# Split weights stored in device memory and fetched again as parts, in a kernel of attention and two feed-forward layers

## The chip, the cores and the metric

One Trainium2 chip, one NeuronCore. The metric is the device time of one execution in microseconds (us): 1044.35 us for the kernel before, the median of three runs. Five engines take part. TensorE (PE, with its weight loads as PEld) multiplies into PSUM banks; VectorE (DVE) and ScalarE (ACT) read those banks; GpSimd (POOL) works on SBUF alone; SyncE (SP) issues nearly all DMAs, in the order in which they stand in its program. Every engine takes its own instructions in order, so one that waits holds up all that stand behind it.

## The reference, cut to what matters

```
scores = scale * q @ k.T + decay           # 4 batches, 8 heads, 576 rows, head size 64
attn   = softmax(causal(scores)); x = attn @ v        # 2304 tokens, 512 wide
xn     = x / sqrt(mean(x*x) + 1e-6) * rms_g
x      = (silu(xn @ w_gate) * (xn @ w_val)) @ w_out   # 512 -> 1536 -> 512
out    = silu(x @ w_in) @ w_out2                      # 512 -> 2048 -> 512
```

The inputs q, k, v, f and rms_g are float32. The five weight matrices come as float64, which no engine multiplies: the kernel turns each 64-bit word into a float32 by integer operations ("decoding").

## The kernel before, in words

Every product of the two layers is made to nearly float32 accuracy from two parts of each operand, a high part (h) and the rounding rest, the low part (l): three matmuls, h by h, l by h and h by l, add up in one PSUM bank (`terms`, line 720). In names of tiles the last letter tells the part (`b11h`, `t4l`), and weights are `wh`, `wl` (input side) and `woh`, `wol` (output side).

The program runs in five stages. Attention comes first. Then each of the two layers goes over the tokens in two phases, tokens 0 to 1279 and 1280 to 2303: stage 2 is the gated layer's first phase, stage 3 its second, stage 4 the second layer's first phase, stage 5 its second. In each stage the loop `for g in range(0, NF, G)` of `layer` takes two column blocks of 128 at a time; such a step is called a group here. The gated layer has six groups in a stage, each with two input weights (gate and val), and the second layer eight groups, each with one. Stage 2 multiplies plainly. Stages 3 to 5 take a 2 by 2 block scheme with seven products (`p1`, `p2`, `p6`, `p5`, `p7`, `p4`, `p3`), for which the weights' four blocks `a11, a12, a21, a22` and four sums of blocks (`s1` to `s4`) are wanted; the first half of the group uses the tiles with `a11, a12, s2, s1` (here the first part) and the second half those with `a21, a22, s3, s4` (the second part). In stage 3 a group's order on PE is: 12 matmuls of p1, 12 of output blocks, p2, output, p6, output, p5, output, p7, p4, p3. "Output blocks" are the multiplications by `woh` and `wol` of the group before, which are put off into the next group (`pending`).

In the products, ACT copies a bank three times while it goes on filling (line 732: `u1` after p1, `u2` after p6, `u3` after p7, and p4 can only go on after the copy of `u3`); DVE adds such copies to other banks (line 737); ACT applies silu (line 830); DVE or POOL multiplies gate by val (line 837); ACT and DVE split the result (lines 639, 640).

Weights come in through `weights`: the first time, a 512 KB DMA into a tile `st`, one ACT and four DVE operations (lines 143 to 147) and a store of the float32 block to a `kept` tensor in device memory; the second time, a DMA of the `kept` block. After that, every time, `unit_in` makes the four sums on POOL (line 162), the high parts on ACT (165) and the low parts on DVE or POOL (166); `unit_plain` (183, 184) and `unit_out` (193, 194) do the same without sums. So in stages 3 and 5, where weights come the second time, sums and splits are made anew. `unit_ahead` decodes blocks of `w_in` during stage 3: eight of its sixteen (`AHEAD_OF`).

Buffers that set the order: four tiles each of `wh` and `wl`, three each of `woh` and `wol`, three tiles `f` for weights in float32, nine tiles `c`. The order of each engine's instructions is set when the program is built, by a scheduler that works with its own estimates; waits on semaphores keep it right at run time.

## Time and profile before

| | us |
|---|---|
| median of three runs (lowest to highest) | 1044.35 (1044.26 to 1046.67) |
| the profiled execution, whole | 1049.42 |
| its span, first to last instruction | 1047.6 |
| PE busy in the span | 1027.0 (98%) |
| DVE, ACT, POOL busy | 762.8, 566.0, 408.7 |
| stages 1 to 5, by the profiled execution | 224.7, 239.1, 191.1, 211.4, 181.3 |
| DMA moved | 104.29 MB, mean 100 GB/s |

A busy PE is not yet a PE at its pace: matmuls overlap, and the profile models their ends. What PE loses is seen better where two starts stand farther apart than usual, and in the list of what ended its waits. In the notation, "PE t L720 <- ACT c L732: 3.0, 3, 1.5" says that matmuls of line 720 into a tile `t` waited for ACT's writing of `c` in line 732, 3.0 us in total, three times, 1.5 us at the longest. PEclk is the granted share of TensorE's full clock.

### The profile page before, as it was taken

Reading aid. Unit: us, or ns where it says so; the run is one execution under the profiler, and the core shown is the slowest. Engines: PE = TensorE matmul, PEld = TensorE weight load, DVE = VectorE, ACT = ScalarE, POOL = GpSimd, SP = SyncE. Lnnn points to the kernel's source line nnn. Section 1 sums busy time; section 2 is a strip of 40 time slices with the busy share of each in tenths; the row PEclk is TensorE's granted clock in tenths of the full one; section 3 lists DMA queues with packets and bytes.
Section 4 is the critical chain, followed back from the end, with each engine's and each line's share of the span. In section 5 each row is a group of like instructions: output and inputs, shape, how many; then the busy total and the mean of one; then the engine's idle time right before and its main releaser. Section 6 shows DMA issues by size and latency. Waiting matters only on the chain.

```text
span 1047.6 us, 16037 instructions
## 1 busy us (share of the span) xinstructions
PE 1027.0 (98%) x5459; PEld 848.8 (81%) x5459; DVE 762.8 (73%) x1509; ACT 566.0 (54%) x1191; POOL 408.7 (39%) x601
## 2 busy tenths in 40 slices
PE   8999999999999999999998999999999999999998
PEld 7877777778788888888787887887787888888886
DVE  6889887877666767976487657968887697366664
ACT  6998888883442322534544454664444465544441
POOL 7776766511111216323344635235534322222300
PEclk8999999999999999999999999999999999999999
DMA  6464543112432524231333312134442233111102
GB/s 145 132 182 121 137 107 92 36 62 100 142 109 74 162 79 151 71 111 35 117 111 115 107 50 81 61 121 151 151 142 91 81 121 131 51 52 70 51 1 80
DMA packets 113008, 104.29 MB, mean 100 GB/s; under 512 B 62768, under 2 KB 83664, under 8 KB 112928
## 3 DMA queue, kind: packets, MB, share of 16 engines
q1 hardware_dynamic: 111200, 100.14, 31.2%
q10 hardware_dynamic: 1728, 3.15, 1.0%
q8 instruction: 43, 0.70, 0.3%
q14 instruction: 37, 0.30, 0.1%
HBM read 77.49 MB, written 25.76 MB: 99 GB/s over the span
## 4 chain that ended last, share of the span: by engine, by line
PE 78%; DVE 10%; ACT 4%; issue 3%; POOL 3%; DMA 1%; POOLq 0%; SPq 0%; DVEq 0%; ACTq 0%
PE t L720 33%; PE s L720 17%; PE x L720 13%; PE s L449 5%; PE o L501 4%; PE t L473 3%; POOL f L162 2%; ACT pr L464 1%; PE s L408 1%; DVE xa L897 1%; DVE hl L640 1%; DVE c L737 1%; DVE f L146 1%; ACT g L264 1%; PE s L290 1%
## 5 line engine op out<-in xcount | busy, mean ns | idle before, releaser
L194 POOL TENSOR_TENSOR wol<-c,woh 128x512 fp32r<-128x512 f32 x54 | 76.7, 1427 | 282.1 <-ACT woh L193 254.6
L640 DVE TENSOR_TENSOR hl<-c,hh 128x512 fp32r<-128x512 f32 (+1 forms) x140 | 112.1, 808 | 53.1 <-ACT hh L639 52.9
L162 POOL TENSOR_TENSOR f<-f 128x256 f32<-128x256 f32 x112 | 88.7, 813 | 134.2 <-DMA f<-keptb 54.5
L639 ACT ACTIVATE hh<-c 128x512 fp32r<-128x512 f32 (+1 forms) x140 | 79.5, 583 | 62.0 <-DVE c L837 24.2
L436 POOL TENSOR_SCALAR dt<-ncb,c8t 128x64 f32<-128x64 f32 (+2 forms) x144 | 79.5, 555 | 41.6 <-DVE nm L452 34.5
L732 ACT ACTIVATE c<-t 128x512 f32<-128x512 f32 x84 | 49.6, 590 | 72.5 <-PE t L720 72.3
L464 ACT ACTIVATE pr<-pr,nm 128x192 f32<-128x192 f32 (+3 forms) x144 | 80.2, 558 | 12.5 <-DVE nm L452 10.3
L830 ACT ACTIVATE c<-c 128x512 f32<-128x512 f32 x66 | 41.6, 630 | 80.5 <-DVE c L737 80.5
L166 DVE TENSOR_TENSOR wl<-f,wh 128x1024 fp32r<-128x1024 f32 (+1 forms) x48 | 60.6, 1270 | 31.0 <-ACT wh L165 31.0
L452 DVE CUSTOM_DVE_ANT_0 pr<-s,dt 128x256 f32<-128x256 f32 (+7 forms) x160 | 69.5, 450 | 18.5 <-PE s L449 7.4
L165 ACT ACTIVATE wh<-f 128x1024 fp32r<-128x1024 f32 (+1 forms) x56 | 54.1, 975 | 41.4 <-POOL f L162 21.7
L473 PE MATMUL t<-ident,pr 128*128 128x128 f32 x384 | 69.1, 280 | 2.2 <-ACT pr L464 1.6
L184 POOL TENSOR_TENSOR wl<-f,wh 128x1024 fp32r<-128x1024 f32 x12 | 28.7, 2392 | 95.3 <-ACT wh L183 77.5
L720 PE MATMUL s<-hh,woh 128*128 128x512 f32 (+1 forms) x172 | 64.9, 377 | 0.3 <-DVE xa L879 0.3
L720 PE MATMUL s<-hl,woh 128*128 128x512 f32 (+1 forms) x172 | 64.6, 375 | 0.0
L720 PE MATMUL s<-hh,wol 128*128 128x512 f32 (+1 forms) x172 | 64.5, 375 | 0.0
L737 DVE TENSOR_TENSOR c<-t,c 128x512 f32<-128x512 f32 x60 | 41.3, 688 | 30.6 <-ACT c L732 16.5
L830 ACT ACTIVATE c<-t 128x512 f32<-128x512 f32 (+1 forms) x74 | 37.5, 511 | 40.4 <-PE t L720 38.8
L897 DVE TENSOR_TENSOR xa<-x,xa 128x512 f32<-128x512 f32 x64 | 43.6, 681 | 21.1 <-PE x L720 21.1
L879 DVE TENSOR_TENSOR xa<-s,xa 128x512 f32<-128x512 f32 (+1 forms) x72 | 45.7, 640 | 18.2 <-PE s L720 18.0
L720 PE MATMUL x<-wol,hh 128*128 128x512 f32 (+1 forms) x146 | 57.1, 391 | 1.8 <-POOL wol L194 1.8
L720 PE MATMUL x<-woh,hh 128*128 128x512 f32 (+1 forms) x146 | 56.8, 389 | 0.0
(231 smaller groups left out, 3209.8 us busy)
## 6 DMA issues: line engine op xcount, KB each, us to landing
st<-in_moe_w_out_dram SPq DMA_DIRECT2D x28, 512.0 KB, 3.8
st<-in_moe_w_in_dram SPq DMA_DIRECT2D x16, 512.0 KB, 3.8
st<-in_moe_w_gate_dram SPq DMA_DIRECT2D x12, 512.0 KB, 3.8
kepta<-f SPq DMA_DIRECT2D x24, 256.0 KB, 2.2
st<-in_moe_w_val_dram SPq DMA_DIRECT2D x12, 512.0 KB, 4.3
f<-kepta SPq DMA_DIRECT2D x24, 256.0 KB, 2.7
f<-keptb SPq DMA_DIRECT2D x24, 256.0 KB, 2.6
out_dram<-xa SPq DMA_DIRECT2D x17, 256.0 KB, 2.0
```

Source lines behind the costliest of these rows:

```text
L162: nc.gpsimd.tensor_tensor(out=out_, in0=x, in1=y, op=op)
L165: nc.scalar.activation(out=hi[i][:, u], in_=f[i][:, u], func=AF.Copy)
L166: (nc.gpsimd if plain and i else nc.vector).tensor_tensor(out=lo[i][:, u], in0=f[i][:, u], in1=hi[i][:, u].bitcast(F32), op=ALU.subtract)
L194: nc.gpsimd.tensor_tensor(out=lo, in0=f, in1=hi.bitcast(F32), op=ALU.subtract)
L436: nc.gpsimd.tensor_scalar(out=dt, in0=p.nct[:, 0 if last else D :][:, :n], scalar1=c8t[:, c, p.i : p.i + 1], scalar2=1.0, op0=ALU.add, op1 ...
L452: nc.vector.tensor_tensor_reduce(out=self.pr[:, ks], in0=sp, in1=self.dt[:, ks], op0=ALU.add, op1=ALU.min, scale=-SCALE, scalar=3.0e38, ac ...
L464: e = nc.scalar.activation(out=pr, in_=pr, func=AF.Exp, bias=self.nm, scale=-1.0, accum_out=p.batch.sums[:, self.c, p.hp : p.hp + 1])
L473: nc.tensor.transpose(pt[:, jj * P : (jj + 1) * P], keys[:, jj * P : (jj + 1) * P], ident)
L639: nc.scalar.activation(out=hi, in_=src, func=AF.Copy)
L640: nc.vector.tensor_tensor(out=lo, in0=src, in1=hi.bitcast(F32), op=ALU.subtract)
L720: nc.tensor.matmul(ps, lhsT=l, rhs=r, start=start and z == 0, stop=stop and z == len(mms) - 1, skip_group_check=not (start and stop))
L830: act = nc.scalar.activation(out=hf, in_=a, func=AF.Silu)
```

## The change: what it does

Each weight block is now decoded and split once. Its high and low parts go to device memory (`store`, tensors `half_h_...` and `half_l_...`) and come back from there as ready parts, straight into the tiles that PE reads (`fetch`, used by `units_again` in both second phases and by `unit_out`). The gated layer's sums of blocks are made by a new `unit_sums` from the stored float32 blocks, one group of weights at a time, for gate and val, in the groups that `SUMS_IN` names: three during stage 2 and three during the first three groups of stage 3. It loads two blocks of 256 KB, lets POOL make the four sums, ACT the high part and POOL the low part, and stores four blocks. `AHEAD_OF` now has all sixteen blocks of `w_in` decoded in stage 3, three in each of its first four groups and two in the last two. Half of the second layer's output weights use `wh` and `wl` tiles, which leaves the three `woh` and `wol` tiles to the other half.

```
+SUMS_IN = (2, 3, 4, 6, 7, 8)
+
+AHEAD_OF = ((0, 1, 2), (3, 4, 5), (6, 7, 8), (9, 10, 11), (12, 13), (14, 15))
...
+    def store(key, n, tiles, at_=0):
+        for d, t in zip(kept_halves(key, n), tiles):
+            w = t.shape[-1]
+            nc.sync.dma_start(out=d[:, at_ : at_ + w], in_=t.bitcast(F32))
+
+    def fetch(key, tiles):
+        for d, t in zip(halved[key], tiles):
+            nc.sync.dma_start(out=t.bitcast(F32), in_=d)
...
+    def units_again(keys, m):
+
+        ops = [{} for _ in keys]
+        for i in range(2):
+            for o, key in zip(ops, keys):
+                hi, lo = halves_of()
+                fetch((key, m, i), [flat(t) for t in (hi, lo)])
...
+    def unit_sums(w, key, m):
+
+        f, g = unit_f(w, key, m), plain_half()
+        block_sums([f[:, k] for k in range(4)], {nm: g[:, k] for k, nm in enumerate(SUMS[0] + SUMS[1])})
+        hi, lo = f.bitcast(F32R), g.bitcast(F32R)
+        nc.scalar.activation(out=hi, in_=g, func=AF.Copy)
+        nc.gpsimd.tensor_tensor(out=lo, in0=g, in1=f, op=ALU.subtract)
+        for i in range(2):
+            store((key, m, i), 4 * G2, [flat(t[:, 2 * i : 2 * i + 2]) for t in (hi, lo)], 2 * G2)
...
     def unit_out(w, key, m):
+        if key[0] == "b" and m % 2:
+            both = flat(wip.tile([P, 4, G2], F32R, tag="wh" if m % 4 == 1 else "wl", name="wo"))
+            hi, lo = both[:, :DM], both[:, DM:]
...
+        if (key, m, 0) in halved:
+            fetch((key, m, 0), (hi, lo))
+            return hi, lo
...
-            win = [spread(*((unit_plain, w, f"{n}{z}", g) if plain else (unit_in, w, f"{n}{z}", g, ph == 0))) for z, w in enumerate(w_ins)]
+            if ph:
+                win = units_again(keys, g)
...
+            if n == "a":
+                for w, key in zip(w_ins, keys):
+                    for m in [G * t for t, at_ in enumerate(SUMS_IN) if at_ == ph * NF // G + g // G]:
+                        with tc.issue_after(marks[0]):
+                            unit_sums(w, key, m)
```

Three places in the order of instructions, all in the second group of stage 3 (the numbers in names tell buffers apart; what stands in brackets is what an instruction waits for, DMAHW being earlier DMAs). First SyncE's queue. Before, it holds loads of `kept` blocks, stores of decoded `w_in` blocks and loads of `st`:

```order
L134 DMA f_6748<-kepta0_4_4688 128x512 [waits DMAHW0_49,DMAHW2_49,DVE_49,Pool_49]
L134 DMA f_6749<-kepta0_5_4697 128x512 [waits DMAHW3_49,DMAHW1_49,DVE_49]
L149 DMA keptb0_3_6545<-f_6537 128x512 [waits DVE_49]
L141 DMA st_6799<-in_moe2_w_in_dram 128x4x256 [waits Activation_49]
L134 DMA f_6764<-kepta1_4_4711 128x512 [waits DMAHW6_49,DMAHW4_49,DMAHW2_49]
L134 DMA f_6765<-kepta1_5_4720 128x512 [waits DMAHW0_49,DMAHW5_49,DVE_49,Pool_49]
```

In the changed kernel, the same queue from the loads of the val blocks for `unit_sums` (`f_6970`) to the fetch of the next group's first gate part (`wh_6984`, `wl_6985`) and the store of val's sums:

```order
L154 DMA f_6970<-kepta1_8_5589 128x512 [waits DMAHW4_49]
L132 DMA half_h_a0_8_0_5573<-f_6956 128x512 [waits DMAHW7_49,DMAHW2_49,Activation_49]
L132 DMA half_l_a0_8_0_5574<-f_6959 128x512 [waits Pool_49]
L132 DMA half_h_a0_8_1_5577<-f_6956 128x512 [waits DMAHW3_49,DMAHW1_49]
L132 DMA half_l_a0_8_1_5578<-f_6959 128x512
L154 DMA f_6970<-kepta1_9_5598 128x512
L136 DMA woh_6725<-half_h_ao_3_0_4420 128x512 [waits PE_49]
L136 DMA wol_6726<-half_l_ao_3_0_4421 128x512 [waits DMAHW5_49,PE_49]
L136 DMA wh_6984<-half_h_a0_4_0_4741 128x1024 [waits DMAHW6_49]
L136 DMA wl_6985<-half_l_a0_4_0_4742 128x1024 [waits DMAHW7_49]
L132 DMA half_h_a1_8_0_5604<-f_6970 128x512 [waits DMAHW0_49,Activation_49]
L132 DMA half_l_a1_8_0_5605<-f_6973 128x512 [waits DMAHW1_49,Pool_49]
```

The stores of gate's sums, which wait for POOL's low part, now stand ahead of the second val load and of the fetches for the next group; behind the rows shown come two more stores and the fetch of the next group's val part.

Second, ACT around the copies after p7 (`c_6687` and `c_6697` before, `c_6899` and `c_6909` now). Before:

```order
L732 ACTIVATE c_6687<-t_6547 128x512 [waits PE_49]
L830 ACTIVATE c_6687<-c_6687 128x512 [waits DVE_49]
L732 ACTIVATE c_6697<-t_6556 128x512 [waits PE_49]
L143 ACTIVATE f_6788<-st_6789 128x512 [waits DMAHW7_49,Activation_49]
L830 ACTIVATE c_6711<-t_6547 128x512 [waits PE_49]
```

In the changed kernel:

```order
L798 ACTIVATE c_6899<-t_6759 128x512 [waits PE_49]
L240 ACTIVATE f_6970<-f_6973 128x1024 [waits DMAHW4_49,DMAHW3_49,DMAHW6_49,DVE_49,Pool_49]
L903 ACTIVATE c_6899<-c_6899 128x512 [waits DVE_49]
L798 ACTIVATE c_6909<-t_6768 128x512 [waits PE_49,Activation_49]
L903 ACTIVATE c_6923<-t_6759 128x512 [waits PE_49,Activation_49]
```

The high part of val's sums (`f_6970<-f_6973`, which waits for POOL's sums) has come between the copy for gate and the copy for val.

Third, POOL from the product of gate and val after p2 (`c_6687<-c_6697` stands for the one after p7 before, `c_6899<-c_6909` now). Before:

```order
L162 TENSOR_TENSOR f_6764<-f_6765 128x256 [waits DMAHW6_49,DMAHW5_49,DMAHW2_49]
L162 TENSOR_TENSOR f_6765<-f_6764,f_6765 128x256 [waits DMAHW4_49,DVE_49,Pool_49]
L162 TENSOR_TENSOR f_6764<-f_6764 128x256 [waits Pool_49]
L162 TENSOR_TENSOR f_6765<-f_6764 128x256 [waits Pool_49]
L837 TENSOR_TENSOR c_6687<-c_6697,c_6687 128x512 [waits DVE_49]
L194 TENSOR_TENSOR wol_6777<-c_6778,woh_6776 128x512 [waits DMAHW6_49,PE_49,Activation_49]
```

In the changed kernel:

```order
L241 TENSOR_TENSOR f_6959<-f_6959,f_6956 128x1024 [waits Activation_49]
L181 TENSOR_TENSOR f_6973<-f_6970 128x256 [waits DMAHW5_49,DMAHW4_49,DMAHW6_49,DMAHW3_49,DMAHW7_49,DMAHW1_49,Pool_49]
L181 TENSOR_TENSOR f_6973<-f_6970 128x256 [waits DMAHW6_49]
L181 TENSOR_TENSOR f_6973<-f_6973,f_6970 128x256 [waits Pool_49]
L181 TENSOR_TENSOR f_6973<-f_6970,f_6973 128x256 [waits Pool_49]
L241 TENSOR_TENSOR f_6973<-f_6973,f_6970 128x1024 [waits Activation_49]
L910 TENSOR_TENSOR c_6899<-c_6909,c_6899 128x512 [waits DVE_49]
```

POOL's split of the output weights is gone, its sums are for weights of a later group, and two low parts of 128x1024 have come in.

## Rows read from the trace of the kernel before

**Rows 1.** Five stages: length, busy us (instructions) of each engine, PEclk, DMA share, GB/s
```profile
0.00:224.70 224.70, 217.35 (x1616) 173.03 (x1616) 183.29 (x638) 190.28 (x549) 145.90 (x381) 0.98 0.44 111
224.70:463.80 239.10, 238.36 (x1248) 204.16 (x1248) 174.55 (x295) 95.39 (x166) 56.75 (x35) 1.00 0.35 114
463.80:654.90 191.10, 186.82 (x818) 151.78 (x817) 129.27 (x173) 89.90 (x145) 87.55 (x82) 0.99 0.27 87
654.90:866.30 211.40, 207.15 (x998) 173.30 (x997) 169.79 (x263) 111.81 (x203) 79.64 (x63) 1.00 0.34 114
866.30:1047.60 181.30, 177.31 (x787) 146.55 (x785) 105.86 (x144) 78.63 (x131) 38.84 (x41) 1.00 0.19 63
```
**Rows 2.** Waits of PE, whole span: total us, times, longest
```profile
PE t L720 <- ACT c L732: 3.0, 3, 1.5
PE t L720 <- DVE wl L166: 2.3, 2, 1.4
...
PE x L720 <- POOL wol L194: 1.8, 2, 1.2
...
PE t L720 <- ACT wh L165: 1.3, 1, 1.3
```
**Rows 3.** PE in time, start of stage 3's fourth group: start, us, what, [idle before]
```profile
559.83 0.39 PE L720 MATMUL t<-b11h,wl 128*128 128x512 f32 x1
561.54 0.50 PE L720 MATMUL t<-b11h,wh 128*128 128x512 f32 x1 [1.31 <-ACT wh L165]
...
565.21 0.63 PE L720 MATMUL s<-hl,woh 128*128 128x512 f32 x1
565.64 0.63 PE L720 MATMUL s<-hh,wol 128*128 128x512 f32 x1
```
**Rows 4.** Two groups of stage 3, the third and the fourth, columns as in rows 1
```profile
528.30:558.70 30.40, 30.40 (x133) 24.62 (x132) 22.82 (x31) 12.35 (x20) 17.46 (x16) 1.00 0.40 130
558.70:593.70 35.00, 32.31 (x133) 25.66 (x132) 23.62 (x33) 15.68 (x25) 17.91 (x17) 0.95 0.36 121
```
**Rows 5.** ACT in time in stage 4, a late copy for p4
```profile
725.72 2.00 ACT L165 ACTIVATE wh<-f 128x1024 fp32r<-128x1024 f32 x2 [7.22 <-POOL f L162]
727.63 0.58 ACT L732 ACTIVATE c<-t 128x512 f32<-128x512 f32 x1
```
**Rows 6.** Groups of instructions, whole span: count, busy us, mean ns, idle before
```profile
L194 POOL TENSOR_TENSOR wol<-c,woh 128x512 fp32r<-128x512 f32 x54 | 76.7, 1427 | 282.1 <-ACT woh L193 254.6
...
L162 POOL TENSOR_TENSOR f<-f 128x256 f32<-128x256 f32 x112 | 88.7, 813 | 134.2 <-DMA f<-keptb 54.5
...
L165 ACT ACTIVATE wh<-f 128x1024 fp32r<-128x1024 f32 (+1 forms) x56 | 54.1, 975 | 41.4 <-POOL f L162 21.7
...
L184 POOL TENSOR_TENSOR wl<-f,wh 128x1024 fp32r<-128x1024 f32 x12 | 28.7, 2392 | 95.3 <-ACT wh L183 77.5
```
**Rows 7.** DMA issues, whole span: count, KB of one, us to landing
```profile
kepta<-f SPq DMA_DIRECT2D x24, 256.0 KB, 2.2
...
f<-kepta SPq DMA_DIRECT2D x24, 256.0 KB, 2.7
```
**Rows 8.** Two single us with the DMA engines full, columns as in rows 1
```profile
520.00:521.00 1.00, 1.00 (x6) 0.81 (x5) 0.00 (x0) 0.60 (x1) 0.94 (x1) 1.00 1.05 395
...
721.00:722.00 1.00, 1.00 (x6) 0.84 (x5) 0.93 (x3) 0.00 (x0) 0.00 (x0) 1.00 0.96 322
```
**Rows 9.** POOL in time in stage 3: two sets of four sums
```profile
504.75 2.95 POOL L162 TENSOR_TENSOR f<-f 128x256 f32<-128x256 f32 x4 [6.48 <-DMA f<-kepta]
...
554.99 3.64 POOL L162 TENSOR_TENSOR f<-f 128x256 f32<-128x256 f32 x4 [2.02 <-issue]
```
**Rows 10.** DVE in time: the same operation, with POOL idle, and beside POOL's sums
```profile
721.11 0.43 DVE L145 TENSOR_SCALAR f<-f 128x512 int32<-128x512 int32 x1
...
556.04 0.85 DVE L145 TENSOR_SCALAR f<-f 128x512 int32<-128x512 int32 x1
```
**Rows 11.** SyncE's queue in time in stage 3's third group
```profile
546.10 5.97 SPq L654 DMA_DIRECT2D t<-c x3
```

More of the change, by code (lines that the diff above doesn't have):

```diff
@@ L118, in block_kernel, with kept_halves @@
     kept = {}
+    halved = {}
+    def kept_halves(key, n):
+        if key not in halved:
+            halved[key] = [dram.tile([P, n], F32, name="_".join(map(str, ("half", z) + key))) for z in "hl"]
+        return halved[key]
+    def store(key, n, tiles, at_=0):
[5 more added lines that the diff above has]
+            nc.sync.dma_start(out=t.bitcast(F32), in_=d)
+    flat = lambda t: t.rearrange("p a f -> p (a f)")
     def plain_half():
@@ L147, in weights, with blocks @@
         nc.vector.scalar_tensor_tensor(out=wi, in0=low, scalar=29, in1=wi, op0=ALU.logical_shift_right, op1=ALU.bitwise_or)
-        kept[key] = dram.tile([P, n], F32, name="kept" + "_".join(map(str, key)))
-        nc.sync.dma_start(out=kept[key], in_=w)
-    def unit_in(w, key, m, plain):
+        if keep:
+            kept[key] = dram.tile([P, n], F32, name="kept" + "_".join(map(str, key)))
+            nc.sync.dma_start(out=kept[key], in_=w)
+    SUMS = (("s2", "s1"), ("s3", "s4"))
+    def blocks(hi, lo, names, n):
+        return {nm: tuple(t[:, n + k].rearrange("p (c f) -> p c f", f=P) for t in (hi, lo)) for k, nm in enumerate(names)}
@@ L161, in unit_in @@
-        for out_, x, y, op in ((s1, a21, a22, ALU.add), (s2, s1, a11, ALU.subtract), (s3, a11, a21, ALU.subtract), (s4, a12, s2, ALU.subtract)):
-            nc.gpsimd.tensor_tensor(out=out_, in0=x, in1=y, op=op)
-        for i in range(2):
-            u = slice(0 if plain or not i else 1, 4)
-            nc.scalar.activation(out=hi[i][:, u], in_=f[i][:, u], func=AF.Copy)
-            (nc.gpsimd if plain and i else nc.vector).tensor_tensor(out=lo[i][:, u], in0=f[i][:, u], in1=hi[i][:, u].bitcast(F32), op=ALU.subtract)
@@ new lines, in unit_in @@
+        for i in range(2):
+            hi, lo = halves_of()
+            nc.scalar.activation(out=hi, in_=f[i], func=AF.Copy)
+            (nc.gpsimd if i else nc.vector).tensor_tensor(out=lo, in0=f[i], in1=hi.bitcast(F32), op=ALU.subtract)
+            store((key, m, i), 4 * G2, [flat(t) for t in (hi, lo)])
+            ops |= blocks(hi, lo, (("a11", "a12"), ("a21", "a22"))[i] + SUMS[i], 0)
+        return ops
+    def units_again(keys, m):
+        ops = [{} for _ in keys]
+        for i in range(2):
+            for o, key in zip(ops, keys):
+                hi, lo = halves_of()
+                fetch((key, m, i), [flat(t) for t in (hi, lo)])
+                o |= blocks(hi, lo, (("a11", "a12"), ("a21", "a22"))[i] + SUMS[i], 0)
+        return ops
@@ L194, in unit_out @@
         nc.gpsimd.tensor_tensor(out=lo, in0=f, in1=hi.bitcast(F32), op=ALU.subtract)
+        store((key, m, 0), DM, (hi, lo))
         return hi, lo
```

46 lines of the change are left out of this document (31 added, 15 removed).

## The prediction

> **What bounds the kernel now.** I read the busy time by stage first. In [rows 1] the reader sees PE busy for 97 to 100 per cent of every stage, and no other engine near it: from stage 2 on DVE, the next with work of its own, has 174.55 of 239.1 us, 129.27 of 191.1, 169.79 of 211.4 and 105.86 of 181.3. DMA is a quarter to a third busy after attention. So work taken from DVE, ACT or POOL is worth nothing in itself; the change can gain only where PE waits for weights, and lose only where it makes new waits.
>
> The list of what ended PE's waits [rows 2] gives all of that: 3.0 us for the copies in `c`, 2.3 for `wl`, 1.8 for `wol` and 1.3 for `wh`, 8.4 us in 8 waits. The timeline [rows 3] shows how a wait is counted: the 0.39 us of the matmul before it is a modelled end, while 133 matmuls of a steady group take 30.40 us [rows 4], 0.229 us from start to start. Each wait costs some 0.16 us more than its idle time, 1.3 us for all eight. The same rows show one thing more. After the pauses of 559 to 565 us the starts stand 0.43 us apart (565.21 and 565.64), not 0.23, and the group's mean granted clock is 0.95 [rows 4]: PE runs at its lower level (1.2 in place of 2.4 GHz) for some time. Seven such starts, 0.2 us each, are 1.4 us. So 8.4 + 1.3 + 1.4 = 11.1 us are all that the weights can cost in this profile.
>
> **What is taken away.** The waits lie as follows: about 1.1 us in stage 3's third group and 4.4 us, slow clock included, at the start of its fourth, where POOL and ACT had to make sums and high parts anew and came late [rows 3]; in stage 4 two late copies before p4 and one `wol`; in stage 5 one `wol`. Stage 4's copies come late because ACT makes two high parts of 2.00 us just ahead of the copy that p4 needs [rows 5]. There the weights come the first time and are still decoded and split, but eight of the sixteen blocks that were decoded in stage 4 are now decoded a stage earlier, and in the new order no high part stands directly in front of these copies. One copy, worth 0.46 us, waits for no weight; I leave it in. **Removed: 11.1 - 0.46 = 10.6 us.** That is the sum if nothing new is late.
>
> **Work that only moves off or onto covered engines.** By the counts of the two orders POOL makes 80 sums of weights in place of 112, 32 x 0.813 = 26 us less [rows 6]; 28 of 54 low parts of output weights go, less 28 x 1.427 = 40 us; twelve low parts of 128x1024 come, at the 2392 ns that the nearest row has, 28.7 us more. Net: 37 us less. ACT's high parts of 128x1024 (975 ns) go from 56 to 28, and DVE's low parts of input weights from 48 to 8. Decoding is the same in sum, but eight blocks of `w_in` move from stage 4 to stage 3. All this costs or gives nothing, since PE covers it; without that cover the moved decoding would be eight times one ACT and four DVE operations, which at 0.43 to 0.85 us each [rows 10] is 2 to 4 us a block.
>
> **DMA in stage 3.** This is what has to pay. By the order, SP's queue goes from 99.8 MB in 421 DMAs to 196.3 MB in 677, and stage 3 has the worst of it: fetched parts are twice as large as the float32 blocks (2 MB in place of 1 MB for a group's input weights and the same again for its sums), three blocks of `w_in` per group come in at 512 KB and go out at 256 KB, and the sums of a later group cost 1 MB in and 2 MB out. Between the fetches of two successive groups' first parts the queue holds 10.22 MB for group 2, 8.91 for group 3, 9.96 for group 4 and 7.6 for group 5, against 130 GB/s x 30.4 us = 4.0 MB in the old third group [rows 4]. Two microseconds with the DMA engines full moved 395 and 322 GB/s [rows 8]. So 10.22 MB take 25.9 to 31.7 us; I take 370, between the two, which gives 27.6 us in a group of 30.4. It just fits, if the queue never stands.
>
> The Trainium skill, page "DMA: Bandwidth & Descriptors", section "Specifications", gives a limit of about 358 GB/s for one core's share of HBM; by it the estimate for 10.22 MB is 28.5 us. The 395 GB/s of this trace [rows 8] are above that figure, and there the trace decides.
>
> But it stands. The stores of the sums wait for POOL and ACT, and stand ahead of the next loads. That a waiting DMA holds this queue the row shows where SP stood for 5.97 us [rows 11]. I walk through group 2, from its first matmul (t = 0):
> - the fetch for its second part can start when the tiles are released, at about -1.4, and 4.46 MB later the last load for gate's sums is in: -1.4 + 12.0 + 2, the last as landing time between 2.2 and 2.7 [rows 7], = 12.6;
> - POOL's four sums 2.95 us [rows 9], to 15.6; ACT's high part 1.0, to 16.6; POOL's low part 2.39, to 19.0;
> - the store of it, then the second load for val: 22.6; sums to 25.5; ACT's high part to 26.5.
>
> In the new order of ACT that high part stands **in front of the copy of val's bank after p7**. Silu and the copy, some 0.6 us each [rows 5], end at 27.7, while p4 for val wants it at about 26.5 (p7 ends after nine of eleven parts of 2.72 us, at 24.5, p4 of gate and matmuls of p3 fill the time to then). So PE waits 1.2 us. With sums of 3.64 us [rows 9], taken beside DVE's decoding, it is 2.6; two sets would make it so. I take 2.0, as much decoding lies there.
>
> The doubling in [rows 10], 0.43 us of DVE alone and 0.85 beside POOL's sums, is contention by this trace. The Trainium skill, "GPSIMD Engine Reference", section "Specifications", says that POOL shares its SBUF interfaces with VectorE; by it the later of the two figures, 2.6 us, would be the one to expect. The trace agrees with it in both rows.
>
> Group 3 is the same with other data ahead: POOL's block differences of tokens are stored first, behind which SP stands as in [rows 11], until about 19.3. The sums' load is in at 22, sums 25 to 25.6, high part 26 to 26.6, the copy after it 26.6 to 27.2, wanted by p4 at 24.5: 2.1 to 2.7 us, or nothing if the scheduler's slack of some 3 matmuls more is there. I take 2.0 of 0 to 2.7. The first group comes out with some 2 us to spare, and later groups have no sums.
>
> **The starts of groups 3 and 4.** Their first parts stand behind loads of output weights that wait for PE's release of `woh` at 21.8; 3.67 MB behind that are 9.9 + 2 us, in at 33.7 for a group that starts at 30.4. Between p1 of gate and p1 of val the order has output blocks, which need only what came earlier, so that the wait is 0 to 2 us; I take 0.7. Pauses of this size let the clock fall once in the old profile; I take half of it, 0.7.
>
> **The rest.** Stage 2 and the start of stage 3 get stores of parts and three sets of sums, with DVE, ACT and POOL at 73 per cent or less [rows 1] and no wait of PE in the list: +0.3, between -1.5 and +2, since no row shows a stage 2 whose loads stand behind stores. In stage 4 nothing new is late: its loads of `st` come a group ahead. In stage 5 a group fetches 3.15 MB (input parts and two output pairs), 8.5 us of DMA at 370 GB/s in 181.3 / 8 = 22.7 us [rows 1], with two sets of tiles, and without any sum or split: no wait, which takes the old `wol` one away. Attention is unchanged.
>
> **Sum.** New in stage 3: 2.0 + 2.0 + 0.7 + 0.7 = 5.4; with 0.3 elsewhere 5.7. Net: 5.7 - 10.6 = -4.9 us. Against the profiled execution's own 1049.42 (span 1047.6) that is 1044.5. That execution lies 5.07 us above the median of the runs, 1044.35; I carry the difference over and forecast **1039.5 us** for the median.
>
> **The rivals.**
> - *All is hidden* (1033.8): the loads run at 395 GB/s and more and the scheduler's slack covers the copies. For it: 98 per cent of PE busy was kept with worse before. Against: 10.22 MB in 30.4 us leave 4.5 us even then, and the stores stand longer.
> - *The gain is eaten* (1043.7): copies in two groups at their upper bounds, 2.6 and 2.7, the starts at 2.0 in both groups, the clock's whole 1.4 and some of stage 2's, together 10 in place of 10.6.
> - *Stage 4's waits stay* (1042.5): the high parts are still made there, and if a copy again meets two of them [rows 5], 3 us of the 10.6 aren't won.
> - *Slower: stage 3 is bound by its queue* (1049.8). Place: groups 2 to 4, SP. If loads go at 322 GB/s [rows 8], 10.2 MB take 31.7 us, and SP's standing for POOL's parts adds about 4 us (from POOL's last sum to its low part, 2.39 and 1 for ACT, and some more for a queue that refills): 35.7 for 30.4 us of PE work. Three groups, 5.3 us each, are +16, less 10.6: +5.4. It decides from 10.6 / 3 = 3.5 us a group. For it: a queue at 85 per cent with compute waits in it. Against: the tiles let the queue run about a group ahead, so that a first late group is taken up by what was fetched early.
> - *The change doesn't do what it says*: waits for `wl` in stage 3 would remain if the fetched parts came as late as the made ones. That is the same place and price as the slower case.
>
> **How the numbers follow.** Within 0.3 per cent, about 3.1 us, a measurement here can't tell a change. Chances: the forecast with its own range 1036.5 to 1042.5, 0.44 (0.36 faster, 0.08 within); all hidden 0.14, faster; eaten 0.16 and stage 4's waits 0.06, each within; slower 0.20. Together faster 0.50, same 0.30, slower 0.20. The range reaches from a little below all hidden (half of stage 2's possible -1.5) at 1033.0 to the slower rival, 1050.0.
>
> **What will show it.** In stage 3 the waits for `wl` and `wh` at the start of a group are gone; waits of PE for ACT's `c` stand before p4 in groups 2 and 3, with a high part of sums just ahead of the copy on ACT; DMA moves 250 to 340 GB/s there. Stage 4 has no long copy wait, stage 5 none at all, and attention stays at 224.7. I am wrong if PE waits for fetched `wh` or `wl` for more than 3.5 us in each of three groups of stage 3 (slower), if its clock is below 1.00 in more than one group, if stage 2 grows by over 2 us, or if stage 3's second group shows no late copy.

## The result, and the profile after

The changed kernel takes 1055.32 us, the median of six runs (1052.52 to 1059.08), against 1044.4 us for the kernel before (1044.16 to 1046.67, six runs): 1.0102 times as long, 95% interval 1.0088 to 1.0116. The forecast was 1039.5 us with a range from 1033.0 to 1050.0. It is wrong in sign, and the measured time lies outside the range.

The profiled execution of the changed kernel took 1055.7 us, its span is 1053.9. The execution of before that stands ahead of the prediction was an odd one: in a second one, 1044.05 us long and near the median, the clock was less reduced at the start and the fourth group of stage 3 took 31.1 us, not 35.0 as in [rows 4]. Stages are compared with that second one. The five stages of the kernel before in it (columns as in [rows 1]):

```profile
0.00:222.60 222.60, 215.08 (x1615) 171.11 (x1615) 182.15 (x638) 190.52 (x549) 147.50 (x381) 0.99 0.44 112
222.60:461.70 239.10, 238.36 (x1250) 204.18 (x1248) 174.61 (x295) 95.52 (x166) 56.67 (x35) 1.00 0.35 114
461.70:650.00 188.30, 185.33 (x818) 150.66 (x817) 130.61 (x173) 89.84 (x145) 88.83 (x82) 1.00 0.28 88
650.00:860.90 210.90, 206.93 (x997) 173.34 (x996) 169.87 (x263) 111.82 (x203) 80.04 (x63) 1.00 0.34 114
860.90:1042.30 181.40, 177.33 (x787) 146.58 (x785) 105.22 (x143) 78.55 (x131) 39.67 (x41) 1.00 0.18 63
```

The same stages of the changed kernel:

```profile
0.00:224.90 224.90, 215.32 (x1616) 169.76 (x1616) 182.59 (x638) 190.71 (x549) 147.73 (x381) 1.00 0.48 123
224.90:466.50 241.60, 239.10 (x1249) 204.10 (x1248) 192.13 (x296) 97.39 (x169) 88.22 (x61) 1.00 0.64 214
466.50:667.80 201.30, 189.55 (x818) 154.67 (x817) 119.59 (x181) 76.34 (x129) 65.34 (x54) 0.97 0.78 272
667.80:873.60 205.80, 205.80 (x997) 173.81 (x997) 147.39 (x225) 106.21 (x189) 75.03 (x58) 1.00 0.54 192
873.60:1053.90 180.30, 177.03 (x787) 146.66 (x785) 88.45 (x133) 61.43 (x102) 0.00 (x0) 1.00 0.44 150
```

Line by line: +2.3 in attention, +2.5 in stage 2, **+13.0 in stage 3**, -5.1 in stage 4, -1.1 in stage 5, together +11.6. The gain came where it was expected, with PE busy without a gap in stage 4 by the profile (205.80 of 205.80), and stage 3 took it twice over, though POOL, DVE and ACT are all less busy there than before. What PE waits for in the whole span, to be held against [rows 2]:

```profile
PE t L786 <- ACT c L798: 10.4, 4, 4.4
...
PE x L786 <- POOL wol L259: 1.7, 1, 1.7
...
PE t L786 <- DMA wl<-half_l_a: 1.0, 1, 1.0
```

No wait for a `wh` or `wl` that an engine makes is left. The four waits for the copy in `c` all stand in stage 3 ahead of p4. Its second, third and fourth groups:

```profile
499.40:536.40 37.00, 32.57 (x134) 26.45 (x133) 15.08 (x24) 16.61 (x28) 13.27 (x12) 0.91 0.79 272
536.40:567.00 30.60, 30.24 (x134) 24.70 (x133) 18.21 (x29) 9.34 (x16) 13.21 (x11) 1.00 0.83 288
567.00:604.90 37.90, 33.49 (x133) 26.44 (x132) 22.17 (x34) 11.57 (x20) 14.38 (x11) 0.91 0.81 288
```

Two groups have a granted clock of 0.91. The timeline of PE in the second shows why:

```profile
525.65 0.39 PE L786 MATMUL x<-b22h,wl 128*128 128x512 f32 x1
530.47 0.80 PE L786 MATMUL t<-t4h,wh 128*128 128x512 f32 x1 [4.43 <-ACT c L798]
531.07 0.63 PE L786 MATMUL t<-t4l,wh 128*128 128x512 f32 x1
531.49 0.63 PE L786 MATMUL t<-t4h,wl 128*128 128x512 f32 x1
```

After a pause of 4.43 us the starts are 0.43 us apart in place of 0.23: the lower level, 1.2 GHz, as in [rows 3]. It lasts for eleven starts here and thirteen after the fourth group's pause, 2.4 and 2.8 us. The sixth group has a pause of 2.7 us too, and its granted clock stays at 1.00. Counted from start to start, the four late copies are 4.6, 0.5, 3.2 and 2.7 us; with 5.1 of slow clock, 1.2 for a late fetch at the fourth group's start and 0.5 for an addition they are 17.8 us, against 3.8 us of pauses in the same stage in the second trace of before. The difference, 14.0, is a little more than stage 3's 13.0.

**The late copy, followed back.** ACT in the second group:

```profile
522.68 0.60 ACT L798 ACTIVATE c<-t 128x512 f32<-128x512 f32 x1 [0.76 <-PE t L786]
528.36 1.06 ACT L240 ACTIVATE f<-f 128x1024 fp32r<-128x1024 f32 x1 [5.08 <-DMA wh<-half_h_a]
529.32 0.61 ACT L903 ACTIVATE c<-c 128x512 f32<-128x512 f32 x1
529.84 0.58 ACT L798 ACTIVATE c<-t 128x512 f32<-128x512 f32 x1
```

The copy for gate is at 522.68, the one for val at 529.84. Between them ACT stands 5.08 us in front of line 240, the high part of val's sums. The releaser that is named is most likely not the cause: POOL ends those sums at 528.33, 0.03 us before, and for gate's set ACT also starts 0.03 us after POOL's sums (517.31 after 517.28), with POOL named. POOL in the same group, where a set is the four sums of one weight with their high and low parts:

```profile
514.23 3.05 POOL L181 TENSOR_TENSOR f<-f 128x256 f32<-128x256 f32 x4 [4.32 <-DMA f<-kepta]
...
525.43 2.90 POOL L181 TENSOR_TENSOR f<-f 128x256 f32<-128x256 f32 x4 [4.58 <-DMA f<-kepta]
```

Gate's sums begin 14.8 us into the group, val's 26.0 us; the prediction's walk had 12.6 and 22.6. The second set waits for its second load, and SyncE issues that load (522.23) behind the first set's stores:

```profile
508.98 0.81 SPq L154 DMA_DIRECT2D f<-kepta  x2
...
520.88 0.32 SPq L132 DMA_DIRECT2D half_l_a<-f  x1
...
521.73 0.45 SPq L132 DMA_DIRECT2D half_l_a<-f  x1
522.23 0.44 SPq L154 DMA_DIRECT2D f<-kepta  x1
```

What SyncE's queue stood for from 499 to 604 us, the second to fourth groups:

```profile
SPq L132 <- ACT f L240: 15.5, 4, 6.9
SPq L170 <- DVE f L167: 13.7, 6, 4.6
SPq L132 <- POOL f L241: 7.9, 4, 2.1
SPq L154 <- DMA keptb<-f: 6.7, 2, 5.4
```

These four lines alone are 43.8 of 105 us in which SyncE stands and issues nothing. The Trainium skill, "DMA: Bandwidth & Descriptors", section "Anatomy of one DMA — SWDGE (gpsimd) path", says that DMA engines themselves never wait on semaphores; the wait happens at the issuing sequencer. These lines agree: the stall is shown on SyncE, at the store, and all loads behind it start later.

### The profile page after: what moved, and what is told of

Read it like the earlier page. It is cut to its first block, busy times and chain, and to the rows that moved or that the text cites. A ratio compares the mean times of both kernels' runs of the same rounds, so it can differ in the third digit from the quotient of the medians.

```text
span 1053.9 us, 16231 instructions
## 1 busy us (share of the span) xinstructions
PE 1026.8 (97%) x5459; PEld 849.0 (81%) x5459; DVE 730.1 (69%) x1469; ACT 532.1 (50%) x1135; POOL 376.3 (36%) x553
## 4 chain that ended last, share of the span: by engine, by line
PE 70%; DVE 8%; DMA 7%; POOL 5%; ACT 5%; issue 3%; SPq 1%; ACTq 0%; POOLq 0%; DVEq 0%
PE t L786 28%; PE s L786 15%; PE x L786 13%; PE s L515 5%; PE o L567 4%; PE t L539 3%; DMA wl<-half_l_a 2%; POOL f L241 1%; POOL f L181 1%; DMA f<-kepta 1%; PE s L474 1%; POOL wl L230 1%; ACT pr L530 1%; DMA st<-in_moe_w_gate_dram 1%; DMA half_h_a<-f 1%
## 5 line engine op out<-in xcount | busy, mean ns | idle before, releaser
L181 POOL TENSOR_TENSOR f<-f 128x256 f32<-128x256 f32 x80 | 66.6, 852 | 84.4 <-DMA f<-kepta 38.1
L957 DVE TENSOR_TENSOR xa<-s,xa 128x512 f32<-128x512 f32 (+1 forms) x72 | 46.0, 640 | 24.5 <-PE s L786 24.5
L259 POOL TENSOR_TENSOR wol<-c,woh 128x512 fp32r<-128x512 f32 x18 | 26.4, 1468 | 98.9 <-ACT woh L258 98.9
L975 DVE TENSOR_TENSOR xa<-s,xa 128x512 f32<-128x512 f32 (+1 forms) x63 | 43.2, 685 | 26.2 <-PE s L786 25.6
L910 POOL TENSOR_TENSOR c<-c 128x512 f32<-128x512 f32 x12 | 16.1, 1340 | 102.1 <-DVE c L803 87.3
L786 PE MATMUL t<-t4h,wh 128*128 128x512 f32 x104 | 42.3, 406 | 10.4 <-ACT c L798 10.4
L539 PEld LDWEIGHTS t<-ident,pr 128*128 128x128 f32 x384 | 45.2, 140 | 8.9 <-ACT pr L530 3.6
```

What stands on the lines that cost most here:

```text
L181: nc.gpsimd.tensor_tensor(out=out_, in0=x, in1=y, op=op)
L539: nc.tensor.transpose(pt[:, jj * P : (jj + 1) * P], keys[:, jj * P : (jj + 1) * P], ident)
L786: nc.tensor.matmul(ps, lhsT=l, rhs=r, start=start and z == 0, stop=stop and z == len(mms) - 1, skip_group_check=not (start and stop))
L975: nc.vector.tensor_tensor(out=a, in0=ps, in1=a, op=ALU.add)
```

## The experiments

**What had to be told apart.** Theory A: the new high part has a bad place on ACT, and nothing else. Theory A2: sums that come late hold up everything in order behind them, on SyncE as well as on ACT. Theory B: the bytes are too many. Beside them: F, the shortage of `f` tiles (three, of which a set of sums takes two), and S, the stores in attention. All ratios are to runs of before on the same chip. Most edits also gave the scheduler a new order in other places; where that bears on a reading it is said.

### The kernel before, once more

> The kernel before once more, for a second trace. In the first one the clock was at its lower level from 10 to 20 us and the execution took 5.07 us more than the median of the runs. If that is all the difference, attention takes 224.7 - 2.8 = about 222 us here and the whole about 1046 to 1047. If the changed kernel loses nothing in attention, attention takes the changed kernel's 224.9 us here as well.

1044.05 us, attention 222.6. In its first 25 us the granted clock is 0.93 here and 0.86 in the first trace. So the changed kernel's attention, 224.9 with 1.00 there, is longer by 2.3 us and by more at an equal clock.

### Bytes without arithmetic

```
-        f, g = unit_f(w, key, m), plain_half()
-        block_sums(...)
-        nc.scalar.activation(out=hi, in_=g, func=AF.Copy)
-        nc.gpsimd.tensor_tensor(out=lo, in0=g, in1=f, op=ALU.subtract)
+        f = unit_f(w, key, m)
+        hi = lo = f
```

> unit_sums makes no sums and no parts: the two loads of a weight are followed by four stores of what was loaded, so the same bytes go through the same queue, but no store waits for POOL or ACT (the sums' values are wrong by that). Theory A2 (SP stands for the sums, and with it all loads behind): stage 3 at 187 to 190, with 2 us or less of waits, and a run of 1041 to 1044. Theory B (the bytes are too many for the time): stage 3 still at 196 to 201, 1051 to 1055.

1044.11 us. Stage 3:

```profile
465.90:655.90 190.00, 186.30 (x818) 151.91 (x817) 119.75 (x182) 72.70 (x125) 36.80 (x30) 0.99 0.78 277
```

This version leaves out the sums and the split into parts, and stores what it has loaded. Stage 3 takes 190.0 us in place of 201.3, with 277 GB/s in place of 272, and the late copies in the second and fourth groups are gone; what remains is 1.9 us for fetches at the fourth group's start and 2.2 at the last p4, where A2 had allowed 2 in all. So **it is not the bytes** alone: the same loads and stores fit when no store waits for an engine. A2 stands. A and F are not excluded, since the run also takes the high part off ACT and one of a set's two `f` tiles away. The whole gains little on the kernel before, since attention took 226.5 us in it; to that I come back.

### All sums in stage 2

```
-SUMS_IN = (2, 3, 4, 6, 7, 8)
+SUMS_IN = (1, 2, 3, 4, 5, 5)
```

> SUMS_IN is (1, 2, 3, 4, 5, 5): all sums are made in stage 2, none in stage 3. Theory A: only the waits behind the sums go, groups 2 and 3 of stage 3, -7.5 us; the late copies in the fourth group (3.2 us, DVE) and at the sixth group's end (2.7) stay; stage 2 grows by 0 to 3: 1048 to 1051. Theory B: with 3 MB less in each of three groups all of stage 3's waits go, some 16 us with the slow clock, stage 2 grows by 0 to 3: 1039 to 1043.

1057.12 us, 1.0115 (1.0099 to 1.0132). Stages 2 and 3:

```profile
225.30:482.30 257.00, 244.86 (x1247) 208.65 (x1247) 188.91 (x288) 103.13 (x175) 117.48 (x87) 0.97 0.67 226
482.30:667.70 185.40, 183.77 (x818) 151.02 (x817) 123.05 (x190) 70.82 (x123) 36.20 (x28) 1.00 0.73 261
```

Stage 3 without sums is at 185.4 us, 2.9 less than before: fetching ready parts does there what it was meant to, with sixteen decoded blocks beside it. It is 15.9 us shorter than in the changed kernel, which is B's number (16) and not A's (7.5); but the bytes and the arithmetic left the stage together, so this run doesn't choose between B and late sums. Both theories were wrong on stage 2, which pays 15.4 us more than in the changed kernel. The sums cost about as much in either stage. There PE waits for POOL's low part of output weights (3.4 us), for DVE's product of gate and val (4.2) and for the norm (2.9); what each of them stood behind I did not follow.

### The high part on POOL

```
-        nc.scalar.activation(out=hi, in_=g, func=AF.Copy)
+        nc.gpsimd.tensor_copy(out=hi, in_=g)
```

> The high part of the sums (line 240) is made by POOL in place of ACT; nothing else changes. Theory A (ACT stands at that high part, behind it the copy that p4 needs): the late copies in stage 3's second and third groups go, 4.6 + 0.5 us with 2.4 us of slow clock after the first: 1055.3 - 7.5 = about 1048. Theory B (the DMA queue is so full that the sums, decoded blocks and fetches come late wherever they are used): the waits come back at other places of the same groups, 1053 to 1056.

1085.37 us, 1.0388 (1.0371 to 1.0405): far from both. The copy before p4 in the second group isn't late any more, but the standing has moved with the instruction, and the scheduler put POOL's work in stage 2 in another order, the output weights' low parts behind the sums. PE waits for output weights in stage 2, because POOL stands for the load of the sums in front of their low part:

```profile
PE x L786 <- POOL wol L259: 15.4, 3, 9.4
```
```profile
352.45 2.89 POOL L181 TENSOR_TENSOR f<-f 128x256 f32<-128x256 f32 x4 [7.65 <-DMA f<-kepta]
355.41 1.04 POOL L240 CAST f<-f 128x1024 fp32r<-128x1024 f32 x1
356.52 2.34 POOL L241 TENSOR_TENSOR f<-f 128x1024 fp32r<-128x1024 f32 x1
358.82 2.49 POOL L259 TENSOR_TENSOR wol<-c,woh 128x512 fp32r<-128x512 f32 x2
```

The POOL time that is added, 1.04 us a set, is little; behind the longest wait of PE, 9.4 us, stand these 7.65 us of waiting in order. The rest of the 30 us was not followed.

### The high part held back

```
-        nc.scalar.activation(out=hi, in_=g, func=AF.Copy)
+        with tc.issue_after(after) if after else ExitStack():
+            nc.scalar.activation(out=hi, in_=g, func=AF.Copy)
...
-                            unit_sums(w, key, m)
+                            unit_sums(w, key, m, marks[2] if ph and key == "a1" else None)
```

> In stage 3 the high part of val's sums is held on ACT until gate's silu after p4, so that it stands behind both copies that p4 needs; all else is as in the changed kernel. Theory A (only the place on ACT is at fault): the 4.6 us wait of the second group and its 2.4 us of slow clock go, and stage 3 is 7 to 8 us shorter, 193 to 195. Theory A2 (the late sums hold up everything behind them): the low part and its stores come some 5 us later still, and the fetches behind them in SP's queue with them, so that the wait goes to the start of the third group, for wh or wl: stage 3 at 199 to 205.

1052.09 us, 1.0072 (1.0047 to 1.0096); stage 3 196.9, between the ranges of the two. Its second and third groups:

```profile
498.40:528.70 30.30, 30.21 (x134) 24.70 (x133) 14.20 (x24) 15.09 (x27) 7.97 (x7) 1.00 0.88 305
528.70:566.00 37.30, 32.42 (x133) 25.66 (x132) 22.56 (x33) 11.67 (x19) 19.33 (x16) 0.95 0.80 290
```

Where the held high part stood, the wait is gone (37.0 to 30.3 us), which is A, though val's sums are later still: their high part starts 35.2 us after the group's start, in place of 29.0, since both of val's loads stand behind gate's stores in this order. In the next group it is back (30.6 to 37.3): there a high part, by its place that of gate's sums, runs at 558.06 us, after ACT stood 3.83 for POOL's sums, and p4's copy behind it at 559.54. That is A2, with the place that I had not named: not a fetch at the third group's start (1.0 us only), but again ACT. The order on ACT makes a late set into a late p4; why sets are late is another matter, and the next ones come late as well.

### One set of sums in a group

```
-SUMS_IN = (2, 3, 4, 6, 7, 8)
+SUMS_IN = ((1, 2, 3, 4, 6, 8), (2, 3, 4, 5, 7, 9))
...
-                for w, key in zip(w_ins, keys):
+                for z, (w, key) in enumerate(zip(w_ins, keys)):
```

(and `SUMS_IN[z]` in the line below it.)

> The sums of gate and of val are made in different groups, never two sets in one: gate's in groups 1, 2, 3, 4, 6 and 8, val's in 2, 3, 4, 5, 7 and 9, counted from stage 2's first as 0 (6 to 9 are stage 3's first four). Theory F (the second set of a group comes late since it waits for the f tiles and for SP behind the first set's stores): with one set, its high part on ACT stands some 10 us ahead of p4's copy, the 4.6 us and the slow clock of stage 3's second group go, and stage 3 takes 190 to 194 in place of 201.3. Theory B (too many bytes): the bytes are the same in all, stage 3 at 198 or more.

1052.62 us in one run; stage 3 191.3, within F's 190 to 194, and the second group 30.1 us. The expectation is wrong on one point: in stage 2, groups 2 to 4 still have a set of gate and one of val each. Only stage 3 has one set a group, and it has four sets in place of six. There the high part stands 4.8 us ahead of the copies after p7, no longer between them:

```profile
523.44 1.06 ACT L240 ACTIVATE f<-f 128x1024 fp32r<-128x1024 f32 x1 [2.75 <-POOL f L181]
...
528.25 0.60 ACT L798 ACTIVATE c<-t 128x512 f32<-128x512 f32 x1 [0.76 <-PE t L786]
```

So, with the trace of the changed kernel, it is the **second set of a group**, behind the first one's stores, that comes late; that fewer sets in stage 3 also help is not excluded. Stage 2, which now has eight sets in place of six, and some of them in its second and last groups, takes 247.3 us, 5.7 more than in the changed kernel; that gives back more than half.

### Stores of sums on other queues, and sums in `c` tiles

```
-            store((key, m, i), 4 * G2, ..., 2 * G2)
+            for d, t, e in zip(kept_halves((key, m, i), 4 * G2), (hi, lo), (nc.scalar, nc.gpsimd)):
+                e.dma_start(out=d[:, 2 * G2 :], in_=...)
```

> The stores of the sums are issued by ACT (high parts) and POOL (low parts), each behind the operation that makes the data, so that SP stands for none of them; arithmetic and bytes are the same. Theory A2: the 15.5 + 7.9 us that SP stood for them from 499 to 604 us become loads that start earlier; of stage 3's 13 us at least 8 go: 1045 to 1048. Theory A (the high part's place on ACT alone): the sums' loads come no earlier, 1053 to 1057.

1063.13 us, 1.0161 (1.0127 to 1.0195). Slower, where A2 as I had put it asked for faster. SyncE issued val's second load some 4 us earlier in the group than in the changed kernel, at 520.8, but POOL's sums began only when the first set had been stored out of the tile that they write:

```profile
530.39 2.88 POOL L181 TENSOR_TENSOR f<-f 128x256 f32<-128x256 f32 x4 [4.62 <-DMA half_h_a<-f]
```

The two stores of gate's high part, which ACT issued at 521.9 and 522.3, took 6.6 to 7.8 us to land, where those of the changed kernel took 2.4. The late copy grew to 8.8 us. So earlier loads do not help as long as the second set has to wait for the first one's tiles, which is F. The changed kernel has both holds: in its stage 3's second group the load behind the stores ends the wait, but in stage 2 val's sums wait in each of the three groups for the first set's store, 5.0, 3.4 and 4.2 us, as here:

```profile
311.44 3.19 POOL L181 TENSOR_TENSOR f<-f 128x256 f32<-128x256 f32 x4 [4.97 <-DMA half_h_a<-f]
```

Which of the two holds costs more is not shown.

```
-        f, g = unit_f(w, key, m), plain_half()
+        f = unit_f(w, key, m)
+        g = [late["tmp"].tile([P, DM], F32, tag="c", ...) for _ in range(2)]
```

> The changed kernel with the sums written to two tiles c instead of a tile f, so that a set holds one of the three f tiles, not two, and the next set and the decoded blocks need not wait for its stores. Theory F: the second set's sums in stage 3's second group are done 3 us earlier or more, the 4.6 us wait at p4 goes: stage 3 at 190 to 195. If SP's order alone decides, the second load still stands behind the first set's stores: stage 3 at 198 to 203.

(The high and the low part of a set are made in two halves each here.) 1066.79 us in one run, stage 3 204.9. The second group's late copy shrank to 0.4 us, but the scheduler had also put the sets elsewhere, and with two of nine `c` tiles taken PE waits for other things (3.8 us for an addition of DVE, 2.6 for a split of ACT). This run can't tell F from a new order. A fourth tile `f`, which would, was not tried.

### Eight blocks of `w_in` ahead

```
-AHEAD_OF = ((0, 1, 2), (3, 4, 5), (6, 7, 8), (9, 10, 11), (12, 13), (14, 15))
+AHEAD_OF = ((0, 1), (2, 3), (12, 13), (14, 15), (), ())
```

> AHEAD_OF as in the kernel before: eight blocks of w_in are decoded in stage 3 and eight in stage 4. Theory A: the late copies of groups 2 and 3 stay; stage 4 gets its two late copies back (+3 to 4.4 us): 1055 to 1059. Theory B: 0.77 MB less for each of eight blocks in stage 3 takes the waits of the fourth and sixth groups away (3.2 + 2.6 of slow clock + 2.7), stage 4 gives back 3 to 4.4: 1049 to 1052.

1062.19 us, 1.0165 (1.015 to 1.018), worse than both. Stage 3 gives 2.9 us (198.4): the late copies of the fourth and sixth groups go, as B had it, but 4.5 us for a fetch and 2.2 for a copy come at the third group's end. Stage 4 takes 215.2, 9.4 more than in the changed kernel and 4.3 more than before; neither theory had that.

### The second layer only

```
+            if first:
+                store((key, m, i), 4 * G2, [flat(t) for t in (hi, lo)])
...
-            if ph:
+            if ph and n == "b":
                 win = units_again(keys, g)
+            elif ph:
+                win = [spread(unit_in, w, key, g, False) for w, key in zip(w_ins, keys)]
```

(the gated layer without stores of parts and without `unit_sums`.)

> Only the second layer's weights are stored as parts and fetched again; the gated layer's weights are kept in float32 and their sums made anew in stage 3, as in the kernel before; sixteen blocks of w_in are decoded in stage 3 and half of the output weights use the wh and wl tiles, as in the changed kernel. By the stages of the second trace of before (222.6, 239.1, 188.3, 210.9, 181.4) and of the changed kernel (224.9, 241.6, 201.3, 205.8, 180.3), theory 1 (the gated layer's stores, sums and fetches make all of the loss, in stages 1 to 3): stages 1 and 2 as before, stage 3 at 188 to 190, stages 4 and 5 as in the changed kernel: 1042.3 - 5.1 - 1.1 = 1036 of span, 1038 of time. Theory 2 (the eight blocks of w_in more in stage 3 are at fault): stage 3 stays above 195, 1044 or more.

> The same with AHEAD_OF as in the kernel before, eight blocks in stage 3 and eight in stage 4. If decoding in stage 4 is what makes its late copies: stage 4 at 211 to 215 as in the run with eight blocks ahead, 1042 to 1047. If the stores of parts in stage 4 do it, both of these runs have them and differ by under 2 us.

1048.97 us with sixteen blocks, 1.0032 (1.0019 to 1.0045), and 1047.43 with eight, 1.0017 (1.0007 to 1.0027). Stages 3 and 4, first with sixteen, then with eight:

```profile
463.80:659.30 195.50, 188.02 (x818) 151.66 (x818) 147.28 (x203) 94.26 (x155) 87.02 (x80) 0.99 0.40 131
659.30:866.30 207.00, 205.89 (x997) 173.81 (x996) 147.22 (x225) 106.04 (x189) 74.32 (x58) 1.00 0.54 191
```
```profile
463.70:652.40 188.70, 185.58 (x819) 150.65 (x818) 132.43 (x175) 91.46 (x148) 87.19 (x80) 1.00 0.31 99
652.40:865.10 212.70, 208.09 (x997) 174.79 (x996) 167.88 (x257) 109.14 (x197) 72.58 (x58) 0.99 0.56 197
```

Theory 2 was right about stage 3: eight blocks more cost 6.8 us there and give 5.7 in stage 4, with sums on POOL and splits on DVE still in place and the DMA engines 40% busy. So the decoding that was moved at no cost has a price beside such work. With all sums in stage 2 sixteen blocks stood in a stage 3 of 185.4 us, so the price hangs on what else is in the stage. That stage 4 is at 212.7 with eight, within the 211 to 215 that were asked for, shows that it is mostly decoding that makes the late copies there: storing parts is the same in both runs. Both runs spend 180.3 to 180.6 us in stage 5, a gain of some 1.0: that is all that ready parts are worth there.

### Attention, and a version meant to be faster

```
+        def stores():
...
+        stores() if done[0] else waiting.append(stores)
```

(`waiting` is run behind the first group's text.)

> The changed kernel with the parts of the first group's weights, made during attention, stored in stage 2's first group; all else as it was. Theory S: attention 3 us shorter at an equal clock of the first 25 us (222 to 223 at 0.93, 222 at 1.00), the rest as before within what the scheduler's new order makes of it: 1050 to 1053.

1053.07 us, 1.0076 (1.0053 to 1.01). Attention takes 222.8 us at a clock of 0.93 in its first 25 us, what the kernel before takes at that clock (222.6), and what S had asked for; the run without arithmetic had 226.5 at the same 0.93. The other stages are as in the changed kernel. From 45 to 100 us, in before (second trace), the changed kernel and this one:

```profile
45.00:100.00 55.00, 52.35 (x404) 41.26 (x404) 49.61 (x170) 49.82 (x142) 42.55 (x97) 1.00 0.56 149
```
```profile
45.00:100.00 55.00, 50.48 (x385) 38.78 (x384) 47.53 (x159) 47.57 (x136) 40.29 (x92) 1.00 0.65 183
```
```profile
45.00:100.00 55.00, 52.23 (x405) 41.24 (x404) 49.13 (x171) 49.82 (x144) 42.37 (x98) 1.00 0.65 186
```

The middle one does 19 or 20 matmuls less. But the last moves as many bytes (186 GB/s): the stores did not go to stage 2, as I had expected, they only stand later in the order of the same 55 us (eight stores from 54.6 to 85.1 us in the changed kernel, from 62.7 to 92.7 here). So S met its number by luck and is wrong as it was put. Not the stores cost 2 to 3 us, but the order of SyncE, DVE and ACT that they led the scheduler to. Which instruction of it decides stays open.

> As one_set_a_group, and the parts of the first group's weights, which are made during attention, are stored in stage 2's first group in place of attention. Theory S (the stores between the loads of q, k and v make the loss from 45 to 100 us, where DMA moved 220 in place of 160 to 178 GB/s): attention gets 3 us shorter at equal clock in its first 25 us, 222 to 224. If the loss is not from the stores, it stays at 225 to 228. The whole with stage 3 as above: 1040 to 1046.

1050.8 us, 1.0058 (1.0041 to 1.0075), with nine runs from 1046.28 to 1053.92; its trace is that of the shortest. Attention 223.1, stage 2 245.3, stage 3 189.7. It is the best of the versions that make sums apart, but slower than the 1040 to 1046 that I had asked for, and than before.

> A version meant to beat both: gate's sums in groups 2, 3, 4, 4, 6 and 8, val's in 2, 3, 4, 6, 7 and 9 (none in stage 2's second and last groups, where the runs with one set a group lost 2.9 and 3.4 us), the first group's parts stored in stage 2, and AHEAD_OF as ((0, 1, 2), (3, 4, 5), (6, 7), (8, 9, 10), (11, 12, 13), (14, 15)), a block less in stage 3's third group, which waited for fetches. If the places of the sums are what costs: stage 1 at 222 to 223, stage 2 at 240 to 242, stage 3 at 187 to 190, stages 4 and 5 at 205.8 and 180.5: 1036 to 1041 of span, 1038 to 1043 of time at best, 1041 to 1046 in the median, since the version with one set a group was 4 us slower in its median than in its profile. If each set costs wherever it stands: stage 2 or 3 longer by 5 us or more, 1046 to 1052.

1062.93 us, 1.0152 (1.0125 to 1.0179), a plain miss. Stage 2, one group of which has three sets, took 253.1 us, with PE waiting 3.0 for an addition of DVE, and stage 3 197.1, with 3.4 us for a fetch at the start of the fifth group. No version that computes the whole layer beats the kernel before.

## Why the prediction was wrong, step by step

- **The term of the sum that failed** is "new in stage 3", put at 5.4 us. Pauses and slow clock there came to 17.8 us: 4.6, 0.5, 3.2 and 2.7 for late copies, 5.1 of slow clock, 1.2 for a fetch and 0.5 for an addition, a wait that the kernel before has as well. Attention (2.3) and stage 2 (2.5), put at 0 and 0.3, add to it. The steps behind these terms follow.
- **What bounds the kernel: right.** Less work on POOL (376.3 us busy in place of 408.7), DVE and ACT gave nothing, and the time went where PE waited.
- **Removed, 10.6 us: the mechanism held, the size didn't.** All old waits for made weights are gone, and stages 4 and 5 gave 5.1 + 1.1 us. But 4.4 of the 10.6 stood in a fourth group that took 35.0 us in that execution and takes 31.1 in an ordinary one. The second trace has 7.7 us that are of this kind. I took a sum from a slow execution and took it off the median of others; that alone is 2.9 us.
- **"All this costs or gives nothing, since PE covers it": the step that failed most broadly.** Busy shares of 73 per cent say nothing of work in fixed order that waits for something late. All sums in stage 2 cost 15.4 us more there than half of them, and eight more decoded blocks in stage 3 cost 6.8 us beside sums made anew, with no engine but PE busy for more than 76 per cent of the stage.
- **The walk through group 2: the links that it names held, one was missing, and the sum was too short.** The high part in front of val's copy was the cause as foretold. Wanted at 26.5 after the group's start, the copy ended at 31.0, not 27.7 to 29.1. Gate's sums began 2.2 us late: SyncE stood for 5.4 us because a tile `f` was still being stored (`keptb<-f`), and the loads then took 4.6 us to land. I had costed stores in SyncE's queue and no tile. Val's sums lost 1.2 us more: the second val load was issued 1.4 us after POOL's low part had ended, behind the four stores, and landed 3.2 us later, where the walk had 3.6 for both. Late by 4.6 in place of 2.0.
- **Group 3** had 0.5 us in place of 2.0. **Groups 4 and 6** had 3.2 and 2.7 where the walk said that "later groups have no sums" and stopped. In the fourth, DVE decodes blocks whose loads came late (issued at 582.0 and 583.3, they took 8.7 us to land), in front of the addition that leads to p4's copy:

```profile
591.42 0.43 DVE L164 TENSOR_SCALAR f<-f 128x512 f32<-128x512 f32 x1 [5.22 <-DMA st<-in_moe_w_in_dram]
...
596.15 0.68 DVE L803 TENSOR_TENSOR c<-x,c 128x512 f32<-128x512 f32 x1
```

- **The slow clock**: 5.1 us in place of 0.7. It came after the pauses of 4.6 and 3.2 us, as [rows 3] had shown for shorter ones, but not after the sixth group's 2.7.
- **Starts of groups**: 1.2 us in place of 0.7, right. **Stage 2**: +2.5, 0.5 beyond my end of +2; 1.8 of it is one `wol` that stands behind differences on POOL. **Attention unchanged**: wrong by 2.3. The 224.9 us that were measured lie near the foretold 224.7 by luck: that figure was from an execution with a clock of 0.86 in its first 25 us.
- **The signs of being wrong**: two came, the clock below 1.00 in two groups and stage 2 longer by over 2 us.
- **The rival that came nearest** was the slower one, stage 3 bound by its queue, and its direction was right. It asked for three groups 5.3 us longer each; the second and fourth are 5.7 and 6.8 longer than in the second trace and the third 0.2. But its reason, 322 GB/s, was not it: the bytes fit where no store waits. Its own sign, a wait of over 3.5 us for fetched parts in each of three groups, didn't come either: PE waits for a fetched part once there, for 1.0 us, and the time went to copies on ACT. I had given it 0.20; a queue with compute waits in it, 85 per cent full at 395 GB/s and 91 at the 370 of my sum, should have had the larger share.

## What to carry to other kernels

Work moved beside a full TensorE was not free here where it had a fixed place in front of something that TensorE needs: for each moved instruction, look at what is queued behind it on its engine and at how late its input can be, not at the engine's busy share. A chain of load, compute and store in one queue and few tiles delays a second one that is put into the same group: here val's sums began 11.2 us after gate's. And before a sum of waits is taken from one trace, look at a second execution, or take only waits that the typical time can hold.

## What the hardware showed beside that

An operation of DVE lasted as long as one on POOL beside it. At stage 3's end, first DVE, then POOL:

```profile
657.35 0.68 DVE L706 TENSOR_TENSOR t1l<-xa,t1h 128x512 fp32r<-128x512 f32 x1
...
658.55 2.63 DVE L706 TENSOR_TENSOR t1l<-xa,t1h 128x512 fp32r<-128x512 f32 x1
```
```profile
658.24 2.40 POOL L197 TENSOR_TENSOR wl<-f,wh 128x1024 fp32r<-128x1024 f32 x1 [5.07 <-ACT wh L196]
```

The same subtraction takes 0.68 us alone and 2.63 us beside POOL's; it ends 0.54 us after POOL does. The prediction had counted on twice the time [rows 10], and this is nearly four times. Behind it stand the additions that lead to the last late copy, 2.7 us. The Trainium skill, "GPSIMD Engine Reference", section "Specifications", names the case: POOL shares its SBUF interfaces with VectorE, with contention for DVE instructions with two SBUF inputs. The trace agrees, and gives the size.

Executions of one program differed by more in a version with many stores and fetches: before, 1043.3 to 1047.5 us in one set of twelve, and the version with one set a group and late stores 1046.3 to 1053.9 in nine. The second layer alone, with eight blocks, stayed at 1045.4 to 1049.0 in ten; what makes the difference is not shown.
